# Blockwise causal attention before two MLPs on one Trainium2 core: mask, scale and maximum of the scores in one VectorE instruction, and one buffer of split values less

## Chip, cores and metric

The kernel runs on one core of a Trainium2 chip. The metric is device time in microseconds (us), the median of several runs. Engines are called as in the profile: PE (TensorE matrix products), PEld (its weight loads), DVE (VectorE), ACT (ScalarE), POOL (GpSimd), SP (SyncE, which issues the DMAs).

## What is computed

Attention with a mask by blocks of 64 positions, then two MLPs on all 2304 tokens. Everything is float32.

```
B, H, S, D = 4, 8, 576, 64
scores = q @ k.T / sqrt(D)
scores = where(pos_i // 64 >= pos_j // 64, scores, -1e9)
attn = exp(scores - max(scores)); attn = attn / (sum(attn) + 1e-9)
x = (attn @ v) as 2304 x 512
a = silu(x @ w_gate) * (x @ w_val)      # 512 -> 1536
x = a @ w_out                           # 1536 -> 512
h = x @ w_in                            # 512 -> 2048
out = elu(h) @ w_out2                   # 2048 -> 512
```

## The kernel before

Large products run as three products of split numbers (a high part in a faster format and the rest as a low part), accumulated in PSUM (`mm3`, lines 164 to 166). Weights arrive as 64-bit words and are converted on the chip: `cv_a` on ACT, three integer instructions of `cv_b` on DVE (lines 150, 152, 154), a cast on ACT and a subtraction on POOL.

The program has three parts, which overlap. Up to about 470 us, attention heads and the gate and value products (`gv`, in tokens of 256, nine chunks) are mixed; then comes the product with `w_out` (`y`), then the second MLP (`h` and `o`). Position block 0 of all heads is done apart at the start. The other 512 rows of queries give 64 pieces called heads here (`a_head`, n = 0 to 63): one of 8 heads, one of 4 batches, and one half of 256 queries. A head has two score tiles, `slo` and `shi`, each 128 queries against all keys that any of them may see: 192 and 320 keys in the first half of the sequence, 448 and 576 in the second (`e0`, `e1`). Each score tile has one buffer in PSUM (`slo` one bank, `shi` two), so the next head's product into it waits until the exponential has read it.

For each of the 128 score tiles the order is:

- PE: the product into PSUM (lines 438, 440, 441); the first 8 heads (`fp`) in plain float32, the others as split numbers.
- DVE, `mask` (line 474): a memset of the last 64 columns for the upper 64 partitions to -3e38.
- DVE, `mx` (line 478): the negated row maximum, into one column of `nm`.
- DVE, `sc_nm` (line 481): that column times 1/8.
- ACT, `ex` (line 491): exp(scores / 8 + nm), with the row's sum, into `pl` or `ph` in SBUF; behind it ACT reads the sum's accumulator.

Then DVE makes the reciprocal of the sums (lines 495, 497), ACT (first 20 heads) or DVE (line 503) multiplies, PE transposes blocks of 128 keys (lines 533, 534, 561), ACT copies them as high parts `th` (line 538), DVE subtracts for the low parts `tl` (line 542), and PE multiplies with the values (lines 550, 551, and 574 for the last 64 keys `tt`). The values are split too: for each head from the ninth on, ACT casts them into `vs` (`p_vs`, line 418), POOL writes the rest beside them (line 422). The raw values `rv` of a pair of heads come by DMA. ACT (`xb`, line 584) and DVE (`xf`, line 589) take the result out of PSUM.

What order the instructions have on each engine is decided before the program runs. Every piece of work is added to a `Plan` with an engine, an estimated duration, a priority and the tiles it reads and writes. `Plan.order` plays the estimates through, engine by engine, and the order that comes out is each engine's program; engines run their programs in order. A tag's buffer count in `Plan` (such as `vs=4`) makes the first writer of buffer n wait for every user of buffer n - 4:

```
if tag in self.bufs:
    deps.update(self.users.get((tag, n - self.bufs[tag]), ()))
```

Of the kernel before, what the change touches and what calls it, by code (L numbers as in the profile page):

```python
# [8 lines left out]
F32 = mybir.dt.float32  # L9
# [3 lines left out]
ACTF = mybir.ActivationFunctionType  # L13
ALU = mybir.AluOpType
AXX = mybir.AxisListType.X
AXXY = mybir.AxisListType.XY
PSUM = bass.MemoryType.PSUM
# [93 lines left out]
def attention_moe_moe_kernel(ctx: ExitStack, tc: tile.TileContext,  # L111
# [90 lines left out]
    def pv_t():  # L202
        return at_ps.tile([128, 512], F32, tag="pv", name="pv")


    plan = Plan(dict(raw=2, c=4, rk=2, rq=2, rv=2, ks=3, qh=3, ql=3, vs=4, nm=3, sm=3, pl0=2, pl1=2, ph=2, th=3, tl=3,
                     tt=2, xb=2, xf=2, x=3, slo=1, shi=1, tr=2, pv=1, gv=2, th1=2, s2=2, st=2,
# [3 lines left out]

    pl_t = {g: [attn.tile([128, e], F32, name=f"pl{g}{i}") for i in range(2)] for g, e in ((0, 256), (1, 512))}
    ph_t = [attn.tile([128, S], F32, name=f"ph{i}") for i in range(2)]
    x_p = sb("x", 1)
# [45 lines left out]
    def t0_init():  # L260
        for e, eng, t, k, ns in (("DVE", dve, qz[0], "qz0", 541), ("POOL", pool, qz[1], "qz1", 564), ("DVE", dve, vz, "vz", 1074)):
            for a, b in ((lo_r, hi_r), (hi_r, lo_r)):
                add(e, ns, lambda eng=eng, t=t, a=a, b=b: zero(eng, t, a, b), PT0, writes=[(k, 0, a.start)])
        add("POOL", 900, lambda: make_identity(nc, ident), PT0, writes=[("id", 0, 0)])
        for i in range(2):
            add("POOL", 190, lambda i=i: pool.memset(pl_t[0][i][:, 192:256], 0.0), PT0, writes=[("plz", 0, i)])
            add("POOL", 190, lambda i=i: pool.memset(pl_t[1][i][:, 448:512], 0.0), PT0, writes=[("plz", 1, i)])

    def t0_load_qk(s):
# [121 lines left out]
    def a_head(n, prio):  # L391
# [25 lines left out]
        def p_vs():  # L417
            act.copy(new("vs", 128, 5, 128, bufs=4)[:, 0:nf + 1, 0:64], raws[i][2][:, 0:nf + 1, 64 * j:64 * j + 64])  # L418

# [39 lines left out]
        def qk_hi():  # L459
            sc = sc_hi()  # L460
            if e1 <= 512:
                vw, st["ax"] = [(sc[:, 0, 0:e1], 0)], AXX
                st["shi"] = sc[:, 0, 0:e1]
            else:
                w = e1 // 2
                vw, st["ax"] = [(sc[:, u, 0:w], w * u) for u in range(2)], AXXY
                st["shi"] = sc[:, :, 0:w]
            st["hi_end"] = vw[-1][0]
            for v, o in vw:
                qk(v, 1, o, v.shape[-1])  # L470

        def mask(v):
            w = v.shape[-1]
            dve.memset(v[0:64, w - 64:w], NEG)

        def mx(u):
            v, ax = (st["slo"], AXX) if u == 0 else (st["shi"], st["ax"])
            dve.tensor_reduce(nm_t()[:, u:u + 1], v, ax, ALU.max, negate=True)

        def sc_nm(u):  # L480
            dve.tensor_scalar(st["nm"][:, u:u + 1], st["nm"][:, u:u + 1], SCALE, None, ALU.mult)

# [4 lines left out]
        def ex(u):  # L487
            src, o = st["shi" if u else "slo"], Pt[u]
            if len(src.shape) == 3:
                o = o.rearrange("p (a w) -> p a w", a=2)  # L490
            act.activation(o, src, ACTF.Exp, bias=st["nm"][:, u:u + 1], scale=SCALE, accum_out=sm_t()[:, u:u + 1])

# [12 lines left out]
        for u, e, sk, fn in ((0, e0, slo, qk_lo), (1, e1, shi, qk_hi)):  # L505
            nk, sk2 = ("nm", n, u), ("sm", n, u)
            add("PE", e / (.6 if fp else 1.2) + 10, fn, prio, qk_in, [sk])
            add("DVE", 74, lambda u=u: mask(st["hi_end"] if u else st["slo"]), prio, [sk], [sk])
            add("DVE", 1.04 * e + 68, lambda u=u: mx(u), prio, [sk], [nk])
            add("DVE", 69, lambda u=u: sc_nm(u), prio, [nk], [nk])  # L510
            add("ACT", .833 * e + 240, lambda u=u: ex(u), prio, [sk, nk], [pk[u], sk2])
# [600 lines left out]
```

## Time and profile before

| what | us |
|---|---|
| three timed runs | 1044.62, 1046.24, 1046.64 |
| median | 1046.24 |
| span of the profiled execution | 1045.0 |
| busy PE, DVE, ACT, POOL in it | 1023.0, 825.7, 606.3, 286.5 |

The profile is of one execution; its span runs from the first to the last instruction, and no other time of that execution is given. Busy time of an engine is the time in which at least one of its instructions runs, and durations of matrix products include a modelled end, so a busy PE may still be begun upon too rarely; how many instructions begin in a stretch is the better measure.

### The profile page before, as it was taken

Reading aid. Unit: us, or ns where it says so; the run is one execution under the profiler, and the core shown is the slowest. Engines: PE = TensorE matmul, PEld = TensorE weight load, DVE = VectorE, ACT = ScalarE, POOL = GpSimd, SP = SyncE. Lnnn points to the kernel's source line nnn. Section 1 sums busy time; section 2 is a strip of 40 time slices with the busy share of each in tenths; the row PEclk is TensorE's granted clock in tenths of the full one; section 3 lists DMA queues with packets and bytes.
Section 4 is the critical chain, followed back from the end, with each engine's and each line's share of the span. In section 5 each row is a group of like instructions: output and inputs, shape, how many; then the busy total and the mean of one; then the engine's idle time right before and its main releaser. Section 6 shows DMA issues by size and latency. Waiting matters only on the chain.

```text
span 1045.0 us, 19569 instructions
## 1 busy us (share of the span) xinstructions
PE 1023.0 (98%) x6520; PEld 935.1 (89%) x6520; DVE 825.7 (79%) x1967; ACT 606.3 (58%) x1531; POOL 286.5 (27%) x288
## 2 busy tenths in 40 slices
PE   9999899999999999999999999999999999999998
PEld 8678899999999999999977888898888998898897
DVE  6889999988888888877666775889998666876665
ACT  3898787776776677654354555555563443543343
POOL 1267543443444344303233222223210000000000
PEclk9999999999999999999999999999999999999999
DMA  7577557422542254004779988777646433454331
GB/s 177 163 217 207 154 160 202 122 80 87 139 123 81 85 140 122 25 28 134 227 258 321 316 292 282 252 237 235 218 149 211 126 121 121 122 172 121 112 111 61
DMA packets 119366, 170.00 MB, mean 163 GB/s; under 512 B 15840, under 2 KB 75744, under 8 KB 119264
## 3 DMA queue, kind: packets, MB, share of 16 engines
q1 hardware_dynamic: 119264, 168.74, 53.3%
q8 instruction: 52, 0.85, 0.3%
q14 instruction: 50, 0.41, 0.1%
HBM read 130.42 MB, written 38.27 MB: 161 GB/s over the span
## 4 chain that ended last, share of the span: by engine, by line
PE 79%; DVE 11%; DMA 4%; ACT 2%; issue 2%; SPq 1%; POOL 0%; ACTq 0%; DVEq 0%; POOLq 0%
PE gv L164 8%; PE gv L166 7%; PE gv L165 7%; PE o L893 6%; PE o L892 6%; PE o L891 6%; PE h L165 5%; PE h L166 5%; PE h L164 5%; PE y L165 3%; PE y L164 3%; PE y L166 3%; PE tr L534 2%; PE tr L533 2%; PE pv L551 2%
## 5 line engine op out<-in xcount | busy, mean ns | idle before, releaser
L164 PE MATMUL gv<-xh,wh 128*128 128x256 f32 x864 | 255.8, 296 | 0.2
L165 PE MATMUL gv<-xl,wh 128*128 128x256 f32 x864 | 241.7, 280 | 0.1
L166 PE MATMUL gv<-xh,wl 128*128 128x256 f32 x864 | 241.4, 279 | 0.0
L164 PEld LDWEIGHTS gv<-xh,wh 128*128 128x128 f32 x864 | 163.6, 189 | 4.8 <-issue 3.4
L165 PEld LDWEIGHTS gv<-xl,wh 128*128 128x128 f32 x864 | 163.8, 190 | 0.5 <-DVE xl L604 0.3
L166 PEld LDWEIGHTS gv<-xh,wl 128*128 128x128 f32 x864 | 163.3, 189 | 0.2 <-POOL wl L161 0.2
L853 DVE TENSOR_TENSOR ys<-h,ys 128x384 f32<-128x384 f32 x162 | 88.1, 554 | 69.1 <-PE h L166 66.3
L844 ACT ACTIVATE ar<-ys 128x384 f32<-128x384 f32 x96 | 50.4, 525 | 113.0 <-DVE ys L853 94.9
L165 PE MATMUL h<-yo,ws 128*128 128x384 f32 x326 | 110.1, 338 | 0.6 <-DVE yo L757 0.6
L164 PE MATMUL h<-yo,ws 128*128 128x384 f32 x326 | 109.3, 335 | 0.6 <-ACT ys L864 0.6
L166 PE MATMUL h<-yo,ws 128*128 128x384 f32 x326 | 109.6, 336 | 0.0
L409 POOL TENSOR_TENSOR ks<-rk,ks 64x576 fp32r<-64x576 f32 (+1 forms) x56 | 70.6, 1261 | 90.6 <-ACT ks L406 49.5
L165 PE MATMUL y<-al,woh 128*128 128x512 f32 (+1 forms) x240 | 89.0, 371 | 1.3 <-DVE al L669 1.1
L164 PE MATMUL y<-ah,woh 128*128 128x512 f32 (+1 forms) x240 | 88.5, 369 | 0.2 <-ACT ys L708 0.2
L166 PE MATMUL y<-ah,wol 128*128 128x512 f32 (+1 forms) x240 | 88.4, 368 | 0.0
L803 POOL TENSOR_TENSOR wm<-c,wm 128x256 fp32r<-128x256 f32 x56 | 50.6, 910 | 130.9 <-ACT wm L800 122.9
L538 ACT CAST th<-tr 128x256 fp32r<-128x256 f32 x176 | 61.3, 375 | 24.2 <-PE tr L534 22.8
L542 DVE TENSOR_TENSOR tl<-tr,th 128x256 fp32r<-128x256 f32 x176 | 69.0, 415 | 7.2 <-ACT th L538 6.5
L422 POOL TENSOR_TENSOR vs<-rv,vs 128x320 fp32r<-128x320 f32 (+1 forms) x56 | 47.2, 844 | 96.6 <-ACT vs L418 81.6
L892 PE MATMUL o<-ol,gh 128*128 128x512 f32 x180 | 71.2, 395 | 1.4 <-POOL ol L161 1.4
L893 PE MATMUL o<-oh,gl 128*128 128x512 f32 x180 | 71.5, 397 | 0.8 <-DVE gl L850 0.8
L891 PE MATMUL o<-oh,gh 128*128 128x512 f32 x180 | 70.2, 390 | 0.2 <-ACT oh L157 0.2
(149 smaller groups left out, 2673.5 us busy)
## 6 DMA issues: line engine op xcount, KB each, us to landing
ws<-w_scr SPq DMA_DIRECT2D x168, 256.0 KB, 2.7
w_scr<-wm SPq DMA_DIRECT2D x56, 256.0 KB, 3.9
a_scr<-as SPq DMA_DIRECT2D x54, 256.0 KB, 2.3
ar<-a_scr SPq DMA_DIRECT2D x108, 128.0 KB, 3.7
rk<-in_kt_dram SPq DMA_DIRECT2D x32, 288.0 KB, 4.4
raw<-in_w2i_dram SPq DMA_DIRECT2D x16, 512.0 KB, 4.7
raw<-in_w2o_dram SPq DMA_DIRECT2D x16, 512.0 KB, 4.3
rq<-in_qt_dram SPq DMA_DIRECT2D x60, 128.0 KB, 3.9
```

The costliest lines, as they stand in the source:

```text
L164: pe.matmul(dst, wh, xh, start=start, stop=False)
L165: pe.matmul(dst, wh, xl, start=False, stop=False)
L166: pe.matmul(dst, wl, xh, start=False, stop=stop)
L409: pool.tensor_tensor(st["ks"][64:128, 0:ext], raws[i][0][64:128, j, 0:ext], st["ks"][64:128, 0:ext].bitcast(F32), ALU.subtract)
L538: act.copy(st["th", c], st["tr", c][:, 0:QW])
L542: dve.tensor_tensor(st["tl", c], st["tr", c][:, 0:QW], st["th", c].bitcast(F32), ALU.subtract)
L803: add("POOL", 1000, lambda: pool.tensor_tensor(wm[n][:, 1], part(*x), wm[n][:, 0].bitcast(F32), ALU.subtract), prio, [ck(*x), hk] + whole, ...
L844: add("ACT", 500, lambda: act.activation(t(), src(), ACTF.Tanh, scale=0.5), PMP, [sk], [tk], first)
L853: add("DVE", 560, lambda: dve.tensor_tensor(hc(d), hb[b][:, 0:HT], hc(x), ALU.add), PMP, [hbk(b), hck(x)], [hck(d)])
L891: pe.matmul(d, h, OH[f], start=(p == 0 and u < 2), stop=False)
L892: pe.matmul(d, h, OL[f], start=False, stop=False)
L893: pe.matmul(d, l, OH[f], start=False, stop=(p == HP - 1 and u > 1))
```

## The change

For each score tile the three DVE instructions are replaced by one call. It adds a mask tile `msk` (0, and -3e38 in the upper 64 partitions of its last 64 columns) to the scores, multiplies by -1/8, writes this back over the scores in PSUM, and takes the minimum over the columns into `nm`. The exponential then has the scale -1. `msk` lies in SBUF and is filled once by two memsets on POOL. `Plan` counts the call as 1.04 ns per column and 90 ns, where the three instructions were counted as 1.04 ns per column and 211 ns together. The split values `vs` have three buffers, not four.

```diff
-    plan = Plan(dict(raw=2, c=4, rk=2, rq=2, rv=2, ks=3, qh=3, ql=3, vs=4, nm=3, sm=3, pl0=2, pl1=2, ph=2, th=3, tl=3,
+    plan = Plan(dict(raw=2, c=4, rk=2, rq=2, rv=2, ks=3, qh=3, ql=3, vs=3, nm=3, sm=3, pl0=2, pl1=2, ph=2, th=3, tl=3,
                      tt=2, xb=2, xf=2, x=3, slo=1, shi=1, tr=2, pv=1, gv=2, th1=2, s2=2, st=2,
     pl_t = {g: [attn.tile([128, e], F32, name=f"pl{g}{i}") for i in range(2)] for g, e in ((0, 256), (1, 512))}
+    msk = attn.tile([128, S + 64], F32, name="msk")
...
         for i in range(2):
             add("POOL", 190, lambda i=i: pool.memset(pl_t[0][i][:, 192:256], 0.0), PT0, writes=[("plz", 0, i)])
             add("POOL", 190, lambda i=i: pool.memset(pl_t[1][i][:, 448:512], 0.0), PT0, writes=[("plz", 1, i)])
+        add("POOL", 400, lambda: pool.memset(msk[:, 0:S], 0.0), PT0, writes=[("msk", 0, 0)])
+        add("POOL", 190, lambda: pool.memset(msk[0:64, S - 64:S], NEG), PT0, writes=[("msk", 0, 0)])
...
         def p_vs():
-            act.copy(new("vs", 128, 5, 128, bufs=4)[:, 0:nf + 1, 0:64], raws[i][2][:, 0:nf + 1, 64 * j:64 * j + 64])
+            act.copy(new("vs", 128, 5, 128, bufs=3)[:, 0:nf + 1, 0:64], raws[i][2][:, 0:nf + 1, 64 * j:64 * j + 64])
...
             sc = sc_hi()
             if e1 <= 512:
-                vw, st["ax"] = [(sc[:, 0, 0:e1], 0)], AXX
+                vw = [(sc[:, 0, 0:e1], 0)]
                 st["shi"] = sc[:, 0, 0:e1]
             else:
                 w = e1 // 2
-                vw, st["ax"] = [(sc[:, u, 0:w], w * u) for u in range(2)], AXXY
+                vw = [(sc[:, u, 0:w], w * u) for u in range(2)]
                 st["shi"] = sc[:, :, 0:w]
-            st["hi_end"] = vw[-1][0]
             for v, o in vw:
                 qk(v, 1, o, v.shape[-1])
 
-        def mask(v):
-            w = v.shape[-1]
-            dve.memset(v[0:64, w - 64:w], NEG)
-
-        def mx(u):
-            v, ax = (st["slo"], AXX) if u == 0 else (st["shi"], st["ax"])
-            dve.tensor_reduce(nm_t()[:, u:u + 1], v, ax, ALU.max, negate=True)
-
-        def sc_nm(u):
-            dve.tensor_scalar(st["nm"][:, u:u + 1], st["nm"][:, u:u + 1], SCALE, None, ALU.mult)
+        def mx(u, e):
+            v, m = st["shi" if u else "slo"], msk[:, S - e:S]
+            if len(v.shape) == 3:
+                m = m.rearrange("p (a w) -> p a w", a=2)
+            dve.tensor_tensor_reduce(v, v, m, -SCALE, -NEG, ALU.add, ALU.min, nm_t()[:, u:u + 1])
...
             if len(src.shape) == 3:
                 o = o.rearrange("p (a w) -> p a w", a=2)
-            act.activation(o, src, ACTF.Exp, bias=st["nm"][:, u:u + 1], scale=SCALE, accum_out=sm_t()[:, u:u + 1])
+            act.activation(o, src, ACTF.Exp, bias=st["nm"][:, u:u + 1], scale=-1.0, accum_out=sm_t()[:, u:u + 1])
...
             nk, sk2 = ("nm", n, u), ("sm", n, u)
             add("PE", e / (.6 if fp else 1.2) + 10, fn, prio, qk_in, [sk])
-            add("DVE", 74, lambda u=u: mask(st["hi_end"] if u else st["slo"]), prio, [sk], [sk])
-            add("DVE", 1.04 * e + 68, lambda u=u: mx(u), prio, [sk], [nk])
-            add("DVE", 69, lambda u=u: sc_nm(u), prio, [nk], [nk])
+            add("DVE", 1.04 * e + 90, lambda u=u, e=e: mx(u, e), prio, [sk, ("msk", 0, 0)], [sk, nk])
```

In the compiled program the call is two instructions on DVE: one on the whole tile (ISA with `msk`) and one that writes a column of `nm`.

DVE, the low score tile of the 13th head, before (`c` are weights under conversion, `s` and `as` the gated product, `tt` and `tl` low parts of probabilities, `sm` the sums):

```order
L474 MEMSET slo 64x64
L478 TENSOR_REDUCE nm<-slo 128x1
L150 TENSOR_SCALAR c<-c 128x512
L542 TENSOR_TENSOR tl<-tr,th 128x256
L152 SCALAR_TENSOR_TENSOR c<-raw,c 128x512
L640 SCALAR_TENSOR_TENSOR s_1537<-th_1522,gv 128x256
L568 TENSOR_TENSOR tt<-tr,tt 64x128
L645 TENSOR_TENSOR as<-s_1537,gv 128x256
L154 SCALAR_TENSOR_TENSOR c<-raw,c 128x512
L150 TENSOR_SCALAR c<-c 128x512
L495 TENSOR_SCALAR sm<-sm 128x2
L481 TENSOR_SCALAR nm<-nm 128x1
```

and with the change:

```order
L562 TENSOR_TENSOR tt<-tr,tt 64x128
L639 TENSOR_TENSOR as<-s_1409,gv 128x256
L491 TENSOR_SCALAR sm<-sm 128x2
L477 ISA slo,nm<-slo,msk 128x448
L477 ISA nm 128x1
L536 TENSOR_TENSOR tl<-tr,th 128x256
L493 RECIPROCAL sm<-sm 128x2
L477 ISA shi,nm<-shi,msk 128x2x288
L477 ISA nm 128x1
L583 TENSOR_TENSOR xf<-pv,xb 64x256
L536 TENSOR_TENSOR tl<-tr,th 128x256
```

Between the reduction and its scaling there were nine instructions; now the column of `nm` is written by the next instruction, and the tile of `shi` follows three instructions later.

ACT, the cast of the values of head n = 61 (`vs`), before:

```order
L412 CAST qh<-rq 128x256
L538 CAST th<-tr 128x256
L491 ACTIVATE pl_126,sm<-slo,nm 128x448
L565 CAST tt<-tr 64x128
L491 ACTIVATE ph_128,sm<-shi,nm 128x576
L584 COPY xb<-pv 64x256
L418 CAST vs<-rv 128x5x64
L636 ACTIVATE th_7423<-gv 128x256
```

and with the change:

```order
L487 ACTIVATE pl_126,sm<-slo,nm 128x448
L559 CAST tt<-tr 64x128
L487 ACTIVATE ph_129,sm<-shi,nm 128x576
L630 ACTIVATE th_7340<-gv 128x256
L532 CAST th<-tr 128x256
L578 COPY xb<-pv 64x256
L532 CAST th<-tr 128x256
L420 CAST vs<-rv 128x5x64
```

Before, this 54th cast has 50 copies `xb` ahead of it (one per head, made when a head's last product with `vs` is done); now it has 51, that is one more head is finished first.

## Rows read from the trace of the kernel before

**Rows 1.** The page, busy time by engine; the chain that ended last, by engine.

```profile
PE 1023.0 (98%) x6520; PEld 935.1 (89%) x6520; DVE 825.7 (79%) x1967; ACT 606.3 (58%) x1531; POOL 286.5 (27%) x288
...
PE 79%; DVE 11%; DMA 4%; ACT 2%; issue 2%; SPq 1%; POOL 0%; ACTq 0%; DVEq 0%; POOLq 0%
```

**Rows 2.** Stretches of the span: length; PE, PEld, DVE, ACT, POOL busy (begun); PEclk, DMA share, GB/s.

```profile
20.00:80.00 60.00, 57.42 (x348) 42.04 (x347) 51.04 (x147) 51.01 (x143) 29.12 (x23) 1.00 0.68 189
80.00:140.00 60.00, 54.63 (x416) 51.88 (x416) 58.34 (x131) 46.70 (x116) 37.28 (x31) 0.97 0.64 185
140.00:240.00 100.00, 98.69 (x825) 97.00 (x824) 90.18 (x286) 76.59 (x230) 42.87 (x47) 1.00 0.46 129
240.00:460.00 220.00, 218.16 (x1835) 215.97 (x1834) 188.70 (x616) 149.91 (x457) 85.32 (x93) 1.00 0.34 96
460.00:1045.00 585.00, 575.89 (x3018) 510.77 (x3016) 426.96 (x761) 276.96 (x577) 89.79 (x84) 1.00 0.59 188
```

**Rows 3.** Waits of PE, 20 to 140 us: us in total, times, longest.

```profile
PE pv L551 <- DVE tl L542: 2.6, 6, 0.8
PE slo L440 <- ACT pl L491: 2.1, 1, 2.1
```

**Rows 4.** PE in order of time: start, us, instruction, [idle before, releaser].

```profile
108.48 0.47 PE L440 MATMUL slo<-ks,qh 128*128 128x448 f32 x1 [2.09 <-ACT pl L491]
```

**Rows 5.** DVE in order of time near that wait: start, us, instruction.

```profile
100.38 0.14 DVE L481 TENSOR_SCALAR nm<-nm 128x1 f32<-128x1 f32 x1
100.53 0.11 DVE L474 MEMSET slo<- 64x64 f32 x1
100.67 0.62 DVE L478 TENSOR_REDUCE nm<-slo 128x1 f32<-128x448 f32 x1
101.21 0.42 DVE L150 TENSOR_SCALAR c<-c 128x512 int32<-128x512 int32 x1
...
107.53 0.14 DVE L481 TENSOR_SCALAR nm<-nm 128x1 f32<-128x1 f32 x1
```

**Rows 6.** One stretch behind the wait, as in rows 2; PEclk is third from last.

```profile
110.00:114.00 4.00, 4.00 (x23) 4.00 (x23) 3.85 (x13) 3.76 (x10) 1.28 (x1) 0.63 0.70 238
```

**Rows 7.** Groups by line and shape: busy us, mean ns, idle before and releasers.

```profile
L542 DVE TENSOR_TENSOR tl<-tr,th 128x256 fp32r<-128x256 f32 x176 | 69.0, 415 | 7.2 <-ACT th L538 6.5
...
L422 POOL TENSOR_TENSOR vs<-rv,vs 128x320 fp32r<-128x320 f32 x32 | 31.9, 998 | 53.8 <-ACT vs L418 49.4 <-DMA rk<-in_kt_dram 2.4 <-PE tr L534 1.8
...
L478 DVE TENSOR_REDUCE nm<-shi 128x1 f32<-128x576 f32 x32 | 24.0, 750 | 0.3
...
L481 DVE TENSOR_SCALAR nm<-nm 128x1 f32<-128x1 f32 x128 | 18.2, 148 | 1.6
...
L478 DVE TENSOR_REDUCE nm<-shi 128x1 f32<-128x320 f32 x32 | 15.5, 484 | 0.4
...
L491 ACT ACTIVATION_READ_ACCUMULATOR pl<-slo,nm 128x1 f32 x64 | 12.7, 198 | 0.0
...
L474 DVE MEMSET slo<- 64x64 f32 x64 | 7.2, 112 | 8.2 <-PE slo L438 3.5 <-PE slo L441 1.6 <-PE pv L574 1.1
```

**Rows 8.** The same stretches, the reductions of line 478 alone: DVE busy (begun).

```profile
20.00:80.00 60.00, 10.02 (x21) 1.00 0.68 189
80.00:140.00 60.00, 6.63 (x10) 0.97 0.64 185
140.00:240.00 100.00, 16.56 (x32) 1.00 0.46 129
240.00:460.00 220.00, 36.54 (x67) 1.00 0.34 96
```

**Rows 9.** ACT in order of time: the cast of one head's values.

```profile
426.94 0.46 ACT L418 CAST vs<-rv 128x320 fp32r<-128x320 f32 x1
```

**Rows 10.** PE in order of time: last product of an earlier head, first of that head.

```profile
438.07 0.33 PE L574 MATMUL pv<-tt,vs 128*128 128x128 f32 x1 [0.19 <-DVE tt L568]
...
455.06 0.28 PE L550 MATMUL pv<-th,vs 128*128 128x256 f32 x1
```

More of the change, by code (lines that the diff above doesn't have):

```diff
@@ L15 @@
 AXX = mybir.AxisListType.X
-AXXY = mybir.AxisListType.XY
 PSUM = bass.MemoryType.PSUM
```

## The prediction

> **What bounds the kernel now.** I read the page first, then busy time by stretches of the program, then what TensorE waited for, then single instructions. The page says that PE is busy 98% of the span and that the chain which ended last is 79% PE and 11% DVE [rows 1]. That share is an average over stages, so the question is where the 11% lies. The stretches answer it [rows 2]: what can be read there is busy time and, in brackets, how many instructions were begun. From 240 to 460 us PE begins 1835 matrix products in 220 us, 8.34 per us, and is idle for 1.8 us; the attention heads and the gate/value products are mixed there as they are earlier. From 80 to 140 us it begins only 416 in 60 us. At 8.34 per us those would take 49.9 us, so some 10 us are lost in this stretch, although PE looks 91% busy (its ends are modelled). From 140 to 240 us the same sum gives 825 / 8.34 = 98.9 of 100 us: 1.1 us lost. From 20 to 80 us the first heads run in another form of product, so the counts say little. The engine that is full where PE loses time is DVE: 58.34 of 60 us in 80 to 140, against 189 of 220 us later. There it converts weights for the first MLP beside the heads. What PE then waits for, by name, is DVE's low halves of the transposed probabilities (2.6 us) and once, for 2.1 us, an exponential on ACT [rows 3].
>
> That single wait deserves a closer look. PE stands from 106.4 to 108.48 us before a score product, for lack of the one score buffer of its kind, which `pl L491` has to read first [rows 4]. The exponential needs the scaled maximum. DVE's reduction `L478` for it began at 100.67 us and took 0.62 us; its scaling `L481`, 148 ns of work, began only at 107.53 us, because DVE works in order and other work was queued between the two [rows 5]. The granted clock over 110 to 114 us, right after this pause, is 0.63 of full speed [rows 6], a mean of stretches at 2.4 and at 1.2 GHz: another 0.37 x 4 = 1.5 us of PE. The pause cost some 3.6 us.
>
> **The change, part by part.** There are 64 heads of two score tiles, 128 in all. For each, three DVE instructions go: a memset of 112 ns, a reduction, a scaling of 148 ns [rows 7]. Two come, as the order of instructions shows: the one with the sum, and a read of the accumulator, one column wide.
>
> *The big instruction* reads PSUM and SBUF. The row of that kind, `tl L542`, takes 415 ns for 256 columns: 256 at 1.04 ns and 148 ns. The reductions take 484 ns for 320 columns and 750 for 576, which is 1.04 ns per column and 151 ns [rows 7]. So I count big against reduction as equal. What no row shows is an instruction that also writes all its columns back into PSUM; the low end is no cost, the high end one more 1.04 ns per column. I take the low end, since it is the row nearest in kind; the high end is a rival below.
>
> *The read* has no row on DVE. The nearest is the scaling itself, one column on the same engine, 148 ns; ScalarE's own read of an accumulator takes 198 ns [rows 7]. I take 148, with 0 and 198 as ends. Net per tile: 112 + 148 - 148 = 112 ns less, between 62 and 260.
>
> Are durations the right measure? In [rows 5] the instruction behind the reduction begins at 101.21, 0.08 us before the reduction ends; but the scaling, the memset and the reduction follow each other at 100.38, 100.53 and 100.67, full durations apart. If every removed or added instruction overlapped by 0.08 us, the net gain would be 32 + 68 - 68 = 32 ns per tile. I stay with 112, because the removed ones lie in such a row of dependent work; 32 is a low end. [...]
>
> *What of it counts.* The reductions are placed 21 in 20 to 80 us, 10 in 80 to 140, 32 in 140 to 240, 67 in 240 to 460 (two lie on a border) [rows 8]. In 80 to 140 DVE is full, so all passes on: 10 x 0.112 = 1.1 us. In 20 to 80 DVE is busy 51 of 60 us and ACT just as long; I let half of 21 x 0.112 = 2.4 pass: 1.2 us. From 140 to 460 the saving is 99 x 0.112 = 11 us of DVE, but PE is idle there for 1.3 + 1.8 = 3.1 us only [rows 2], and most of that are waits for other DVE results; a third, 1.0 us.
>
> *The latency.* The scaled maximum now comes with the big instruction; in the new order the read follows it at once, and nothing can be queued between. The pause of 3.6 us arose from just that gap of nine instructions. I count 3.0 us of it, since the contents of the queue ahead of the big instruction can still be late.
>
> *The buffers of split values* are three, not four. Before, the cast of a head's values is released by the last product of the head four earlier, now three earlier. The widest step that I found: the cast for one of the last heads began at 426.94 us [rows 9]; the product that would release it now ended at 438.40, and that head's first product with these values began at 455.06 [rows 10]. Cast and subtraction take 0.5 and 1.0 us on ACT and POOL [rows 7, 9], so 15 us are left: cost nothing. Should that cover go, PE would wait for whatever is over. The raw values are then held as much longer, and their next load on SP's queue waits with them, by the same few us out of those 15. *The mask tile* costs two memsets on POOL at the start, where POOL has to wait for the first converted weights anyway, so nothing. The exponential has another scale and the same shape: nothing.
>
> **The sum:** 1.1 + 1.2 + 1.0 + 3.0 = 6.3 us less. The page gives the profiled execution's span, 1045.0 us, and no time of its own around it; the three timed runs have their median 1.2 us above that span. Behind 460 us nothing is changed and PE is busy 576 of 585 us [rows 2], so I let the gain pass on whole. 1046.24 - 6.3 = 1039.9: I forecast **1040.0 us**. Ends for this case: a read of 0 ns gives 2.6 + half of 5.5 + 3.1 + 3.6 = 12.0, or 1034; a net of 32 ns with the pause back in another place gives 0.3 + 0.3 + 0.3 = 0.9, or 1045.
>
> **The rivals.** *Written back at half speed (slower).* If reading and writing the same PSUM tile costs two cycles per column, each tile grows by its streaming time. That is the reductions' busy time less 150 ns each [rows 8]: 6.9, 5.1, 11.8 and 26.5 us in the four stretches. Less 0.112 per tile this leaves +4.5, +4.0, +8.2 and +19.0 us on DVE. DVE has 9.0, 1.7, 9.8 and 31.3 us idle there [rows 2]. I let pass half, all, half and a third: 2.3 + 4.0 + 4.1 + 6.3 = 17 us, 1063; with the pause shortened all the same, 1060. It decides from 112 ns more per tile, at 384 columns on average 1.33 ns per column instead of 1.04. For it: no row has PSUM on both sides. Against it: DVE's memset of 64 columns into PSUM takes 112 ns, and reductions out of PSUM run at 1.04 ns a column, each side at full rate. The Trainium skill (VectorE: DVE Perf Modes, section The perf-mode tier table) gives two-input work with any PSUM operand one element per cycle, which speaks against this rival; no run here shows it for in-place work. Chance 0.13.
>
> *It isn't one instruction (no change).* If the read costs as much as memset and scaling did, 260 ns, DVE has nothing back. The pause may still shrink, but the whole order of work has moved, and another instruction can come late in its place: 1044 to 1048. For it: PE is 98% busy, and the new order of every engine was made from estimates. Against it: ScalarE's read takes 198 ns, not 260. Chance 0.17.
>
> *A late wait in the new order (slower).* One pause as at 106 us, in another place and without relief on DVE, is +3.6: 1050. Chance 0.07.
>
> **How the numbers follow.** My own case has 0.63. Its upper end lies within 2.1 us of 1046.24 (0.2%, about what can be told from no change) and a little of its chance goes there: faster 0.62, same 0.18, slower 0.20. The range, 1033 to 1053, holds my case, no change and one late wait; it leaves out the half-speed case and a little below.
>
> **What would show it.** Right: big instructions of about 0.35, 0.48, 0.61 and 0.75 us for 192, 320, 448 and 576 columns; reads of at most 0.15 us; DVE some 14 us less busy; no wait of 2 us at a score product near 106 us, and no dip of the clock there; more than 416 products in 80 to 140 us. Wrong: big instructions near 1.3 us for 576 columns; reads of 0.26 us; `vs` waited for by PE; as many products in 80 to 140 us as before.

## The result, and the profile after

The changed kernel takes 1054.01 us (median of 9 runs, 1049.03 to 1056.05); the kernel before, timed beside it on the same chip, 1044.62 us (9 runs). The ratio is 1.0066, with a 95% interval of 1.0039 to 1.0092: slower by 0.66%, some 7 us. (The two medians lie 9.4 us apart; the ratio is the smaller measure, and the one used below.) The forecast was 1040.0 us with a range up to 1053, so the sign was wrong, and the time lies outside the range. The profiled execution took 1055.01 us, its span 1053.2.

The page of the changed kernel, busy time and chain, answers to [rows 1]:

```profile
PE 1025.8 (97%) x6520; PEld 937.5 (89%) x6520; DVE 810.6 (77%) x1839; ACT 606.0 (58%) x1531; POOL 289.8 (28%) x290
...
PE 79%; DVE 9%; DMA 6%; issue 2%; ACT 2%; SPq 1%; POOL 0%; ACTq 0%; DVEq 0%; POOLq 0%
```

DVE has 15.1 us less work (825.7 before) and its share of the chain fell from 11% to 9%; the transfers' share rose from 4% to 6%. The new instruction's groups, by shape, answer to [rows 7]:

```profile
L477 DVE CUSTOM_DVE_ANT_0 shi<-shi,msk 128x576 f32<-128x576 f32 x32 | 24.4, 761 | 0.0
L477 DVE CUSTOM_DVE_ANT_0 slo<-slo,msk 128x448 f32<-128x448 f32 x32 | 19.9, 623 | 2.4 <-PE slo L443 1.3 <-PE pv L568 1.0
L477 DVE DVE_READ_ACCUMULATOR2_ANT nm<- 128x1 f32 x128 | 16.5, 129 | 0.5
L477 DVE CUSTOM_DVE_ANT_0 shi<-shi,msk 128x320 f32<-128x320 f32 x32 | 15.9, 498 | 5.0 <-PE shi L440 5.0
L477 DVE CUSTOM_DVE_ANT_0 slo<-slo,msk 128x192 f32<-128x192 f32 x32 | 11.6, 361 | 6.9 <-PE slo L443 4.3 <-PE slo L440 2.3
```

761 and 498 ns stand against 750 and 484 for the reductions. From 192 to 576 columns the time grows by 400 ns, 1.04 ns per column, as the reduction had it: writing back into PSUM adds nothing per column, and 11 and 14 ns per instruction. DVE in order of time, near 105 us:

```profile
104.66 0.62 DVE L477 CUSTOM_DVE_ANT_0 slo<-slo,msk 128x448 f32<-128x448 f32 x1
105.21 0.14 DVE L477 DVE_READ_ACCUMULATOR2_ANT nm<- 128x1 f32 x1
105.21 0.41 DVE L536 TENSOR_TENSOR tl<-tr,th 128x256 fp32r<-128x256 f32 x1
...
106.28 0.14 DVE L477 DVE_READ_ACCUMULATOR2_ANT nm<- 128x1 f32 x1
106.44 0.42 DVE L583 TENSOR_TENSOR xf<-pv,xb 64x256 f32<-64x256 f32 x1
```

The read is a row of 140 ns, but the instruction behind the first one begins at the same 105.21. In 91 of the 128 tiles the next instruction begins within 20 ns of the read; in the others it begins later, as at 106.44. So in most places the read takes no time of its own, and the call is even a little better than was reckoned. The stretches, as in [rows 2], show where the time went all the same:

```profile
20.00:80.00 60.00, 57.64 (x324) 43.13 (x323) 44.19 (x114) 47.55 (x134) 25.50 (x20) 0.91 0.64 180
80.00:140.00 60.00, 54.02 (x414) 51.20 (x414) 57.58 (x128) 48.62 (x121) 38.83 (x33) 0.97 0.67 186
140.00:240.00 100.00, 98.05 (x820) 96.54 (x819) 86.61 (x252) 75.27 (x227) 42.02 (x46) 1.00 0.46 130
240.00:460.00 220.00, 218.99 (x1847) 216.97 (x1846) 183.53 (x555) 152.91 (x466) 85.28 (x95) 1.00 0.34 97
460.00:1045.00 585.00, 576.06 (x3006) 511.13 (x3006) 424.07 (x757) 274.20 (x573) 95.44 (x84) 1.00 0.59 185
```

From 20 to 80 us PE begins 324 products, not 348. Its clock there is 0.91, 1.00 before; 0.09 of 60 us is 5.4 us, and 24 products are 4.1 us at the rate before, so the clock is enough to account for them. From 80 to 140 us, where 4.1 us of the forecast gain were to come from, there are 414 products (416 before) at the same clock of 0.97. Two places stand out in PE's rows. At the start PE runs dry (its row in order of time, with the idle time before it):

```profile
16.13 0.56 PE L440 MATMUL slo<-rk,rq 64*128 64x192 f32 x2 [1.81 <-DMA rq<-in_qt_dram]
```

and the clock is at 0.57 in the stretch behind it, a mean of both levels:

```profile
16.00:32.00 16.00, 15.83 (x62) 12.82 (x62) 8.70 (x28) 7.63 (x22) 2.87 (x2) 0.57 0.44 113
```

Near 527 us ACT stands 4.5 us for a weight's transfer with a cast `ah` queued behind it, and a `y` product then waits 1.76 us for DVE's `al` (ACT and PE in order of time):

```profile
526.95 0.67 ACT L141 ACTIVATE c<-raw 128x512 f32<-128x512 f32 x1 [4.50 <-DMA raw<-in_w2o_dram]
527.81 0.63 ACT L660 ACTIVATE ah<-ar 128x512 fp32r<-128x512 f32 x1
...
531.05 0.50 PE L164 MATMUL y<-al,woh 128*128 128x512 f32 x1 [1.76 <-DVE al L663]
```

The clock of that stretch is 0.74:

```profile
530.00:535.00 5.00, 3.95 (x12) 3.12 (x13) 4.97 (x7) 2.18 (x5) 2.50 (x2) 0.74 0.72 208
```

The pause at 106 us [rows 4] is gone. In PE's waits, 20 to 140 us, others stand in its place ([rows 3] had 2.6 and 2.1 us):

```profile
PE pv L568 <- DVE tt L562: 3.9, 4, 2.1
PE tr L527 <- DVE tl L536: 1.2, 2, 0.7
```

The longest of them ends at 88.78 us, and the clock is low behind it (PE in order of time, then the stretch):

```profile
88.78 0.47 PE L568 MATMUL pv<-tt,vs 128*128 128x128 f32 x1 [2.11 <-DVE tt L562]
```

```profile
88.00:92.00 4.00, 3.21 (x14) 3.22 (x15) 3.94 (x8) 1.35 (x4) 1.29 (x1) 0.59 0.46 137
```

So a pause of the same length, with a dip of its own, now stands some 20 us earlier. The dip behind the old pause [rows 6] is gone with that pause:

```profile
110.00:114.00 4.00, 3.49 (x29) 3.22 (x28) 3.90 (x9) 3.48 (x10) 2.59 (x2) 1.00 0.64 198
```

### The profile page after: what moved, and what is told of

Read it like the earlier page. It is cut to its first block, busy times and chain, and to the rows that moved or that the text cites. A ratio compares the mean times of both kernels' runs of the same rounds, so it can differ in the third digit from the quotient of the medians.

```text
span 1053.2 us, 19462 instructions
## 1 busy us (share of the span) xinstructions
PE 1025.8 (97%) x6520; PEld 937.5 (89%) x6520; DVE 810.6 (77%) x1839; ACT 606.0 (58%) x1531; POOL 289.8 (28%) x290
## 4 chain that ended last, share of the span: by engine, by line
PE 79%; DVE 9%; DMA 6%; issue 2%; ACT 2%; SPq 1%; POOL 0%; ACTq 0%; DVEq 0%; POOLq 0%
PE gv L163 8%; PE gv L164 8%; PE gv L165 8%; PE o L887 6%; PE o L886 6%; PE o L885 6%; PE h L164 5%; PE h L165 5%; PE h L163 5%; PE y L164 2%; PE y L165 2%; PE y L163 2%; PE tr L528 2%; PE tr L527 2%; PE pv L545 2%
## 5 line engine op out<-in xcount | busy, mean ns | idle before, releaser
L797 POOL TENSOR_TENSOR wm<-c,wm 128x256 fp32r<-128x256 f32 x56 | 55.4, 995 | 131.0 <-ACT wm L794 130.9
L663 DVE SCALAR_TENSOR_TENSOR al<-ar,ah 128x512 fp32r<-128x512 f32 (+1 forms) x60 | 46.3, 773 | 32.5 <-ACT ah L660 24.1
```

The source lines that it names most:

```text
L797: add("POOL", 1000, lambda: pool.tensor_tensor(wm[n][:, 1], part(*x), wm[n][:, 0].bitcast(F32), ALU.subtract), prio, [ck(*x), hk] + whole, ...
```

## The experiments

All were timed in five rounds, beside runs of the kernel before on the same chip. That median was 1046.79 us for e1 to e4, 1047.74 for e5 to e8, 1047.02 for e9 to e12, 1047.22 for e13 to e16 and 1049.33 for e17 and e18, so across groups the ratio is the measure.

### Instruction, order and buffers apart (e1 to e4)

The plan decides the order from its counts, so the new instruction can be run in the old order, and the old three in the new one. e1 has the new instruction planned as the old pieces, two of them empty ("the next run" in its expectation is e3, which has its order and the old instructions):

```diff
-            add("DVE", 1.04 * e + 90, lambda u=u, e=e: mx(u, e), prio, [sk, ("msk", 0, 0)], [sk, nk])
+            add("DVE", 74, lambda: None, prio, [sk], [sk])
+            add("DVE", 1.04 * e + 68, lambda u=u, e=e: mx(u, e), prio, [sk], [nk])
+            add("DVE", 69, lambda: None, prio, [nk], [nk])
```

> The changed instructions and three buffers, but the planner counts each score tile as it did before (three DVE pieces of 74, 1.04 per column + 68, and 69 ns, of which two do nothing). Theory O (the changed kernel is slower because of the order that the new estimates gave): faster than the changed kernel (1054) and some 3 us below the kernel of the next run, which has the same order and the old instructions; if three buffers cost nothing, 1040 to 1044. Theory I (the new instruction itself costs PE time): 1052 to 1056, and slower than the next run. Theory V (the third buffer of split values costs): 1047 to 1053, and the next run as slow or slower.

e2 has memset, maximum and scaling in one planned piece with the count of the change (its mask tile is filled and not read; the definitions of the three, left out here, are those of the kernel before):

```diff
+            def three(u=u):
+                mask(st["hi_end"] if u else st["slo"])
+                mx(u)
+                sc_nm(u)
+
-            add("DVE", 1.04 * e + 90, lambda u=u, e=e: mx(u, e), prio, [sk, ("msk", 0, 0)], [sk, nk])
+            add("DVE", 1.04 * e + 90, three, prio, [sk, ("msk", 0, 0)], [sk, nk])
```

> Memset, maximum and scaling as before, three buffers, one directly behind the other as one piece that the planner counts as 1.04 per column + 90 ns: every engine has the order of the changed kernel, and only the instructions of the score tiles are the old ones (the mask tile is written and not used). Theory O: as slow as the changed kernel or up to 6 us slower, 1053 to 1060. Theory I: near the kernel before, 1043 to 1048. Theory V: 1047 to 1054.

e3 is the kernel before with three buffers of `vs`:

```diff
-... rv=2, ks=3, qh=3, ql=3, vs=4, ...
+... rv=2, ks=3, qh=3, ql=3, vs=3, ...
...
-... new("vs", 128, 5, 128, bufs=4) ...
+... new("vs", 128, 5, 128, bufs=3) ...
```

> The kernel before with three buffers of split values in place of four, nothing else: its order has moved for that reason alone. Theories O and I: 1043 to 1047, no change that can be told. Theory V: 1049 to 1054, that is most of what the changed kernel lost.

e4 is the changed kernel with the one piece counted as the three together:

```diff
-            add("DVE", 1.04 * e + 90, lambda u=u, e=e: mx(u, e), prio, [sk, ("msk", 0, 0)], [sk, nk])
+            add("DVE", 1.04 * e + 211, lambda u=u, e=e: mx(u, e), prio, [sk, ("msk", 0, 0)], [sk, nk])
```

> The changed kernel, with its one piece of work counted as 1.04 per column + 211 ns, the sum that the planner had for the three: another order again, with the same instructions. Theory O, if what matters is only which order happens to come out: anywhere from 1038 to 1054, and its difference to the changed kernel lies in waits that are not at score tiles. Theory I: 1052 to 1056, as the changed kernel. Theory V: as the run with three buffers alone, less 3 us.

| run | us | ratio to before, interval |
|---|---|---|
| e1 new instruction, old counts | 1045.81 | 0.9985, 0.996 to 1.001 |
| e2 old instructions, new count | 1072.25 | 1.0244, 1.0219 to 1.0268 |
| e3 old instructions, three buffers | 1050.21 | 1.003, 1.001 to 1.0051 |
| e4 new instruction, one piece of 211 | 1050.07 | 1.0034, 1.0016 to 1.0052 |

e1 and e3 have the same order on every engine, and so have e2 and the changed kernel. In both pairs the new instruction is the faster one: by 0.4% (1045.81 against 1050.21) in the order of the old counts and by 1.7% (1.0066 against 1.0244) in the new one. The order of the new count costs 0.81% (1.0066 against 0.9985), the order with three buffers 0.3%. In us of 1046: three buffers 3.1 more, the instruction 4.7 less, the count 8.5 more, together the 6.9 of the change. Theory O holds, theory I falls, and V has a part: e3 lies in V's range, e1 between the ranges of O and V. e2 lies above every range (O had at most 1060): in the order of the count of 90 the old three instructions cost more than any theory allowed. The last gate/value product marks the same work in every order; PE's rows in e3, then e1:

```profile
508.94 0.28 PE L166 MATMUL gv<-xh,wl 128*128 128x256 f32 x1
```

```profile
503.85 0.28 PE L165 MATMUL gv<-xh,wl 128*128 128x256 f32 x1
```

In the changed kernel it begins at 513.81, and before at 509.04. In e3 and e1 the clock is 1.00 from 16 to 32 us. So the instruction gives 5.1 us by this point, and all but 1.2 us of the 11.2 by which the spans of the changed kernel and e1 differ (1053.2, 1042.0) are lost ahead of it.

### Repairing the places (e5, e6, e7, e9)

The start and the place near 527 us were repaired in the finished order: single instructions were moved, the plan left as it was.

```diff
+MOVES = ((("xh", 1, 1), ("ex", 0, 0)), (("xl", 1, 0), ("mx", 0, 1)), (("xl", 1, 1), ("mx", 1, 0)))
...
+        for a, b in MOVES:
+            self.move(a, b)
```

That is e5; e6 has `(("ah", 6), ("ca", 38)), (("al", 6), ("cb", 38, 0))` instead, and e7 both. In e6 and e7 the moved cast no longer waits for the last products that read its buffer, so that a part of `y` is computed from another slice; they have that wait less.

> The changed kernel with three instructions moved at the start and nothing else: on ScalarE the fourth cast of the first position block's result (xh) ahead of the first exponential, on VectorE the third and fourth subtraction for it (xl) ahead of the second and third score instruction. Theory P (two places): the loss against the order of the old estimates (8.2 us, 1054.0 against 1045.8) lies mostly in two stalls and the stretches of half clock behind them; the first is here, between 16 and 36 us, and costs about 5 us. Then 1049 us, no stretch near 0.5 of the clock between 20 and 36 us, and products from 40 to 460 us about 5 us earlier than in the changed kernel. Theory D (diffuse): the loss is spread over the whole order, and one place gives less than 1.5 us: 1052.5 or more.

> The changed kernel with one piece moved near 525 us: the cast (ah) and subtraction (al) of the seventh slice of the gated product ahead of the conversion of a second-MLP weight on ScalarE and VectorE, where ScalarE stood for 4.5 us for the weight's transfer. Theory P: the wait of 1.76 us at a y product near 531 us and the dip of the clock behind it (530 to 540 us at 0.83, another 1.7 us) go: 3.5 us less, 1050.5 us; products up to 520 us as in the changed kernel. Theory D: less than 1.5 us, 1052.5 or more, since another late result waits next.

> Both repairs in the changed kernel, five instructions moved in all. Theory P: both gains add up, 5 + 3.5 us: 1045.5 us, the level of the new instruction in the order of the old estimates (1045.8). Theory D: 1051 us or more.

e5 took 1054.32 us (1.0065), e6 1053.18 (1.0059), e7 1054.88 (1.0075): theory P fell, D held. In place of the removed waits others stand. PE in order of time, in e5 and then in e6:

```profile
22.92 0.96 PE L450 MATMUL slo<-rk,rq 64*128 64x192 f32 x2 [0.88 <-ACT pl L497]
```

```profile
524.41 0.80 PE L173 MATMUL y<-ah,woh 128*128 128x512 f32 x1 [0.72 <-ACT ah L670]
```

```profile
525.00:530.00 5.00, 5.00 (x16) 3.98 (x15) 3.52 (x5) 2.05 (x5) 1.88 (x2) 0.64 0.75 260
```

The last row is a stretch of e6: the 1.76 us at 531 are gone, but the low clock only came earlier, 0.64 here. e9 moved PE's own products at the start as well:

```diff
+MOVES = (..., (("gv", 0, 0, 0, 1), ("qk", 1, 0)), (("gv", 0, 0, 0, 0), ("gv", 0, 0, 0, 1)), (("gv", 0, 0, 0, 2), ("qk", 1, 1)), (("gv", 0, 0, 0, 3), ("qk", 2, 0)))
```

> The run with the start repaired, and on TensorE too: the products of the first gate/value tile go ahead of the second head's score products, as they stand in the order of the old estimates (two steps of the contraction ahead of slo, one ahead of shi, one ahead of the next slo). Theory S (the start): the stall of 0.88 us that TensorE met in the run with two engines repaired came from its own order; without it there is no stretch at 0.5 of the clock between 20 and 36 us, products at 140 us begin 4 us earlier than in the changed kernel, and that lasts to the end: 1050 us. Theory D (diffuse): what is gained by 40 us is lost again in later waits: 1052.5 or more.

1056.6 us (1.0086, 1.006 to 1.0112): theory S fell too, and the clock from 20 to 32 us was at 0.50 in its profile. That the low clock at the start isn't a matter of order alone, e10 shows below.

### Which estimates make the order (e10 to e12, e18)

e10 and e11 plan a part of the heads as in e1 and the others as in the change:

```diff
+            if n < 8:
...
+            else:
```

with `n >= 8` in e11. e12 and e18 change the one count to 75 and to 411.

> The new instruction; the first 8 heads (plain float32) counted as three pieces, as before, the other 56 as in the change. The order is that of the run with old estimates up to the eighth head and another one behind it. Theory S: the start as in the old order, so 4 to 5 us less than the changed kernel: 1049 to 1050. Theory D: the start decides nothing; the rest is a new order with its own stalls: 1052 or more, or as low as 1046, with no relation to the start.

> The opposite: the first 8 heads counted as in the change, the other 56 as before. Theory S: the start of the changed kernel, with its half clock between 16 and 36 us, and so 4 to 5 us more than with old estimates alone (1045.8): 1050 to 1051. Theory D: 1046 to 1049, or any other value; the start can be read at 40 us apart from the total.

> The changed kernel with the one number set to what the trace of the changed kernel shows: 1.04 ns per column and 75 ns (from the start of the call to the start of what follows) in place of 90. Theory A (accuracy): the order is worse where the estimates are off; then this one is as good as or better than that of the old estimates: 1045 or less. Theory L (lottery): a change of 15 ns gives just another order among those of 1045.8, 1050.1 and 1054.0 us that this instruction has shown: between 1046 and 1056, not better than the best.

> The changed kernel with the call counted as 1.04 ns per column and 411 ns: in the plan of three pieces the scaled maximum was ready that late, 211 ns of counts and twice the 100 ns that the plan adds between dependent pieces. Theory R (reserve): orders get worse the earlier the plan has the maximum ready (counts of 75, 90 and 211 gave 1056.2, 1054.0 and 1050.1); then this one is at most 1049. Theory L (lottery): any value between 1046 and 1062.

| count of the new call, beside 1.04 ns per column | us | ratio, interval | last gv product |
|---|---|---|---|
| 75 (e12) | 1056.24 | 1.0077, 1.0045 to 1.0109 | 517.27 |
| 90 (the change) | 1054.01 | 1.0066, 1.0039 to 1.0092 | 513.81 |
| 90 for 56 of 64 heads (e10) | 1052.09 | 1.0051, 1.0027 to 1.0075 | 514.49 |
| 90 for 8 of 64 heads (e11) | 1050.98 | 1.0035, 1.0012 to 1.0057 | 513.08 |
| 211 (e4) | 1050.07 | 1.0034, 1.0016 to 1.0052 | 508.73 |
| 411 (e18) | 1050.28 | 1.0019, 0.9991 to 1.0047 | 508.00 |
| three pieces (e1) | 1045.81 | 0.9985, 0.996 to 1.001 | 503.85 |

The truest count gives the worst order of this table: theory A fell, and e12 lies just above theory L's range too. e10 came out as D had it and e11 as S, so the two don't decide about the start. By the ratio each larger count of one piece did better. Neighbours lie within each other's intervals; 75 and 411 differ by 0.58%, more than the 0.43% that their two intervals make together. Of the 0.81% between e1 and the change, 0.49% come with joining the three pieces into one of the same sum, without their hand-overs (e4), and 0.32% with counting that one as 90. e18 missed its bound of 1049 us, beside a kernel before at 1049.33. All this is what theory R says, but a second order at the count of 90 (e16, below) differs from the first by as much as these counts do: R is supported, not shown.

The profiles of e1 and e10 also show what the start is worth. Up to the eighth head their orders are the same, but not the clock. Two stretches of e1 and of e10, then one and the same score product in PE's order of time, again e1 and e10:

```profile
8.00:16.00 8.00, 7.24 (x37) 7.27 (x37) 4.83 (x19) 2.44 (x7) 0.00 (x0) 0.57 1.15 257
16.00:32.00 16.00, 15.56 (x96) 11.45 (x95) 13.41 (x39) 11.13 (x33) 5.10 (x4) 1.00 0.51 135
```

```profile
8.00:16.00 8.00, 6.11 (x51) 5.65 (x50) 6.17 (x24) 3.69 (x9) 0.00 (x0) 1.00 1.17 255
16.00:32.00 16.00, 15.96 (x64) 12.82 (x65) 8.45 (x25) 7.42 (x20) 2.72 (x2) 0.57 0.49 131
```

```profile
36.55 0.59 PE L440 MATMUL slo<-rk,rq 64*128 64x192 f32 x2
```

```profile
40.31 0.59 PE L440 MATMUL slo<-rk,rq 64*128 64x192 f32 x2
```

The same product begins 3.76 us later where the low clock falls behind 16 us, and not ahead of it, where PE waits for transfers anyway (1.46 us for `rq` in e10). The changed kernel's profile has the late form (0.57 behind 16 us). So of the 10 us by which it trails e1's at the last gate/value product, some 4 are the start of that one execution, and some 6 the order behind it; in the table the 513 to 517 us of the last column hold such a start, the 504 to 509 don't (the column is of one execution each; e10's took 1057.59 us, 5.5 above its median). e16, with the count of 90, has 1.00 from 16 to 32 us and begins that product at 519.26; its layout costs at most some 5 us up to there (e17, below), so the low count loses without a late start as well.

The mean granted clock of every timed execution is on record too, and it has a part in the medians. In the 144 executions of the kernel before beside e1 to e18 the time falls by 0.74 us per 0.001 of it (a line fitted to them). The median is 0.992 in the changed kernel's nine executions and 0.995 in e1's twelve. By lines fitted to each kernel's own executions, an estimate, the two take 1051.2 and 1046.1 us at a clock of 0.996: some 5 of the 8.2 us between their medians stay, some 3 go with the clock. Whether the order lowers the clock, or chance did, is not shown.

### Buffers, harmless changes, and the exact old order (e8, e13 to e17)

e8 is the kernel before planned with `vs=3` but built with four tiles. e14 and e15 are the kernel before with the memset's count alone changed, from 74 to 59 and to 89. e13 is e1 with four buffers, so that every engine has the order of the kernel before; for room the mask is in bfloat16, begins in columns that are zero already, and the padding between the SBUF pools is dropped:

```diff
+    big = pl_t[1][1]
+    pl_t[1][1] = big[:, 0:512]
+    msk = big.bitcast(mybir.dt.bfloat16)[:, 896:896 + S]
-    padr.tile([128, 88], F32, name="padr")
+    padr.tile([128, 8], F32, name="padr")
-    x_p.tile([128, 48], F32, name="padx")
-    ph1.tile([128, 80], F32, name="padw")
```

e16 is e13 with the one piece of the change; e17 is the kernel before with that layout.

> The kernel before, planned with three buffers of split values but built with four: every engine has the order of the run with three (1050.2 us), while no cast really has to wait for the product three heads earlier. If the 3.4 us of that run are real waits for a buffer: the level of the kernel before, 1046.8. If they are the other order: 1050.2 again.

> The new instruction with the old counts and four buffers of split values, so that every engine has exactly the order of the kernel before; the mask is kept in bfloat16 behind columns that are zero already, and padding is dropped, so that it fits. Theory O (order costs, instruction gains): the kernel before less the 4.4 us of the instruction in an equal order: 1042.4 us, products between 140 and 460 us about 3 to 5 us earlier than before. Rival: the gain came only in the order of three buffers, which had more slack to take: 1046 to 1047.

> The kernel before with one estimate changed and nothing else: the memset counted as 59 ns, not 74. Instructions, buffers and data are the same; only the order moves, from about 170 us on. Theory L (the old order is a lucky one): any other order costs several us: 1049 to 1054. Theory N (the new call planned as one piece is what makes bad orders): 1046 to 1048, as before.

> The same with the memset counted as 89 ns, 15 more. Theory L: 1049 to 1054 and not the same value as with 15 less. Theory N: 1046 to 1048.

> The changed kernel with four buffers of split values (mask in bfloat16, padding dropped): estimates of the change, no third-buffer limit. If the third buffer has a part in the loss: 3 to 4 us less than the changed kernel, 1050 to 1051. If not: within 2 us of 1054, or another value because this order is again another one.

> The kernel before, same order and instructions, with the SBUF layout of e13 (padding dropped, one tile longer). Theory M (memory layout): the gate/value products take 282 ns, not 279, and the run is 4 to 7 us above the kernel before: 1051 to 1054; e13 (1048.2) is then 3 to 6 us faster than its own pair, which is the instruction's gain in exactly the old order. Rival: the layout does nothing, 1047, and the instruction gains nothing in the old order.

| run | us | ratio, interval |
|---|---|---|
| e8 order of three buffers, four tiles | 1049.6 | 1.0029, 1.0003 to 1.0056 |
| e13 new instruction, exact old order | 1048.2 | 1.0011, 0.9986 to 1.0037 |
| e14 memset counted 59 | 1046.7 | 1.0003, 0.9976 to 1.003 |
| e15 memset counted 89 | 1048.9 | 1.0024, 1.0002 to 1.0046 |
| e16 change, four buffers | 1062.04 | 1.0135, 1.0111 to 1.0158 |
| e17 before, layout of e13 | 1051.63 | 1.0028, 1.0004 to 1.0052 |

e8 equals e3 (1.003): nobody waits for the third buffer; its 0.3% are the order. The two also show how far apart two profiled executions of one order can be: the last gate/value product begins at 512.07 in e8 and at 508.94 in e3. e14 and e15 say how much a shift without meaning does: nothing and 0.24% (e14 as theory N had it, e15 just outside both ranges). The 0.6 to 0.8% of the low counts are more than that. e16 has no limit of three buffers and is slower still (1.0135, of which the layout of e17 explains 0.28%), so lifting the limit does not bring the time back. With the layout's cost taken off, it and the change, two orders of one count, lie 0.4% apart. e13 lies above both values expected for it, in part by its layout. e17 shows a layout cost, though 0.28% is 2.9 us, where 4 to 7 were expected: the groups of gate/value products, 240 to 460 us, in the kernel before and in e17:

```profile
L165 PE MATMUL gv<-xl,wh 128*128 128x256 f32 x400 | 111.6, 279 | 0.0
```

```profile
L165 PE MATMUL gv<-xl,wh 128*128 128x256 f32 x395 | 111.4, 282 | 0.0
```

Against e17, its own pair in order and layout, e13 begins the last gate/value product 5.30 us earlier (e17's row, then e13's):

```profile
514.29 0.28 PE L166 MATMUL gv<-xh,wl 128*128 128x256 f32 x1
```

```profile
508.99 0.28 PE L165 MATMUL gv<-xh,wl 128*128 128x256 f32 x1
```

Most of that is not the instruction's. From 16 to 32 us e17's one profiled execution ran at a lower clock than e13's (e17, then e13):

```profile
16.00:32.00 16.00, 15.52 (x80) 12.10 (x80) 9.63 (x33) 8.12 (x23) 3.05 (x2) 0.77 0.46 124
```

```profile
16.00:32.00 16.00, 15.57 (x94) 11.43 (x93) 13.14 (x39) 11.72 (x35) 5.88 (x4) 1.00 0.56 148
```

How much earlier one and the same product of PE begins with the new instruction, in the two pairs of equal order:

| at (us, in e3 or e17) | e3 to e1, us | e17 to e13, us |
|---|---|---|
| 16 | 0.08 | 1.12 |
| 32 | 0.39 | 4.40 |
| 80 | 1.40 | 5.70 |
| 140 | 1.75 | 3.64 |
| 240 | 4.24 | 4.63 |
| 460 | 5.09 | 5.30 |
| 700 | 4.40 | 2.06 |

From 32 to 460 us the new instruction wins 4.7 us in e1, but 0.9 us in e13, which loses 2.1 us from 80 to 140 us, at a clock of 0.97 (1.00 in e17). At the end of the spans 2.1 us of the 5.3 are left (1050.0, 1047.9). PE's waits from 540 to 640 us, in e13 and in e17, say where the rest went:

```profile
PE y L164 <- DVE al L665: 2.5, 5, 1.2
PE y L163 <- ACT ys L704: 1.5, 1, 1.5
```

```profile
PE y L165 <- DVE al L668: 1.5, 4, 0.8
PE y L164 <- ACT ys L707: 0.3, 1, 0.3
```

2.2 us more of waits in the `y` products are most of the 3.2 us that were lost again. By the ratios e13 is 0.17% faster than e17, which the two intervals do not tell from nothing. No version beats both kernels beyond doubt: e1 is 0.15% below the kernel before, with an interval that holds no change.

## Why the prediction was wrong

**The big instruction**: right. 361, 498, 623 and 761 ns were forecast as 0.35, 0.48, 0.61 and 0.75 us; the rival of half speed is out. The Trainium skill (VectorE: DVE Perf Modes, The perf-mode tier table) gives two-input work with any PSUM operand one element per cycle; the 1.04 ns per column agree, now for work that writes back in place too.

**The read**: 129 ns on the mean, forecast at most 150. As a price it was too much, since in 91 of 128 tiles the next instruction begins with it. The Trainium skill (VectorE: DVE Perf Modes, The DRAIN you can't avoid) has the next operation start when the pipe is empty, and one that is not held start earlier; what begins at 105.21 begins 0.07 us before the call ends, as the second part allows. DVE's busy time fell by 15.1 us, forecast 14. The read of 260 ns, on which the rival "it isn't one instruction" rested, is out; what that rival said of the moved order came true.

**The pause at 106 us** went from its place, with its dip, but one of 2.11 us stands at 88.78 us with a dip of its own. So the 3.0 us counted for it did not come, and 414 products from 80 to 140 us are what the forecast had named as a sign of being wrong. Nor was the pause simply the price of three instructions. e3 has the old three in another order, and in that stretch no wait over 1.0 us and a clock of 1.00:

```profile
80.00:140.00 60.00, 54.72 (x426) 50.84 (x425) 58.63 (x136) 47.05 (x115) 35.48 (x31) 1.00 0.66 186
```

**The sum** of 6.3 us is near what the instruction alone brings in the order of e3, 5.1 us at the last gate/value product and 0.45% or 4.7 us at the end, but by luck. From 80 to 140 us 4.1 us were forecast and 0.35 came; from 140 to 460 us 1.0 us was forecast and 3.3 came; only 20 to 80 us, 1.2 forecast and some 1.3 measured, came out as reckoned. In the exact old order (e17 to e13) the gain is not told from nothing: 0.17%. What I let "pass on whole" behind 460 us did not: in e13 3.2 us of it were lost again, 2.2 of them as waits of the `y` products.

**The buffers**: "cost nothing" holds for waits (e8), as 15 us of cover said. But the planned limit moves the order, and that order costs 0.3% (e3). I costed the wait and not the order.

**The step that failed** is the one that isn't in the sum: the new order of all engines was taken as the old one less the gain. It stood only as the rival "a late wait in the new order", with one pause of 3.6 us and a chance of 0.07, and in the "no change" rival as something that makes up for the gain. Measured, the order of the one piece with its new count costs 0.81%, some 8.5 us, more than the instruction brings; some 3 us of it go with a lower mean clock. It isn't one late wait: removing two of them on up to three engines (e5, e6, e7, e9) gave 0.07% at best. (The pause at 88.78 us was not among them.) The change lowered the plan's count for the maximum by 121 ns, and took out two hand-overs between dependent pieces, for each of which the plan adds another 100 ns (`SELF`); so the plan had the scaled maximum some 320 ns earlier, and the lower that reserve, the slower the kernels were. A likely reason, argued and not shown, is that the plan's other DVE counts are too low: `tl` is counted as 335 ns and takes 415 [rows 7], and the reserve in the scores' counts made up for it.

What stays open: which of the many moved instructions cost the 6 us between 32 and 514 us, whether the late start of the clock comes of the order or of chance, and whether other orders at the other counts would fall on the same line.

## What to carry to other kernels

Where a scheduler works from estimates, a change of an estimate is a change of the whole program: run the new instruction in the old order, and the old one in the new order, before the time is put down to the instruction. More accurate counts are no safe gain as long as the others are off, and the chance of a worse order belongs in the forecast with a size of its own: here 0 to 0.8% for orders that differ in nothing but counts. A repaired wait is worth its length only where nothing else is late just behind it.

## What the runs showed of the hardware

An instruction that reads and writes back the same PSUM tile with a second operand from SBUF ran at 1.04 ns per column, as the reduction did, and the read of its accumulator, a row of 129 ns, delayed nothing in 91 of 128 tiles: the next instruction began with it. Dropping 832 bytes of padding per partition between SBUF pools and lengthening one tile made the gate/value products 282 ns long in place of 279 (in e13, e16 and e17 alike), and the kernel 0.28% slower (e17, interval 0.04 to 0.52). And the same order of instructions ran with the clock at 0.57 either from 8 to 16 us (e1) or from 16 to 32 us (e10), with 3.8 us between the two at 40 us.
